# New durations in a list planner: three chained layers on one NeuronCore

## The chip, the cores and the metric

The kernel runs on one core of one Trainium2 chip. The metric is the device time of one execution in microseconds (us); several runs are summed up by their median. One more execution was profiled, and its trace gives the start and end of every instruction. The engines are TensorE (PE, matrix products), VectorE (DVE), ScalarE (ACT), GpSimd (POOL) and SyncE (SP), which here issues all transfers.

## What is computed

Three layers in a row, all in float32. A retention layer (linear attention whose state decays by a factor per head) takes q, k and v of 4 batches, 8 heads, 768 steps and a head size of 64. Its output, as 3072 tokens of 512 features, goes through two layers that widen to 2048 and come back to 512, the first with h·cos(h), the second with an ELU:

```python
for t in range(S):
    state = gamma[None, :, None, None] * state + np.einsum('bhd,bhe->bhde', k[:, :, t], v[:, :, t])
    y[:, :, t] = scale * np.einsum('bhd,bhde->bhe', q[:, :, t], state)
...
h = x @ w_in            # first layer
x = (h * np.cos(h)) @ w_out
h = x @ w_in2           # second layer
x = np.where(h > 0.0, h, np.exp(np.minimum(h, 0.0)) - 1.0) @ w_out2
```

## The kernel before

**Arithmetic.** Every float32 operand of a large product is split into a high and a low part that PE takes at full rate, and three products of parts (`PARTS`) make one. The splits are a copy on ACT (the high part) and a subtraction on DVE (the low part). The projection back in layer one and both products of layer two use a scheme of seven products on halves of the operands in place of eight, and sums and differences of halves before and after (numbers 1 to 7 in the code).

**Stages in time.** Attention works on 24 units of 128 steps of a batch: `scores` (L536, L547), `carried` (L598) and `values` (L629) are small products of 64 by 64; DVE masks the scores (L563) and keeps the state (L572, L575, L578). They are woven into `hidden`, the first hidden layer (L679, 12 matmuls at a time, up to some 340 us). `project` for layer one follows (L925, to 580 us), then `hidden2`, the second hidden layer (L755, 580 to 820 us), then `project` for layer two (L925, to the end). Weights come as 64-bit numbers and are turned into float32 by two ACT and two DVE steps each half (L374, L377), stored, loaded again and split in `prepare` (L431 for the low part).

**Layer two's hidden stage**, to which the prediction comes most, runs 24 steps, each of seven products of six matmuls. Product sums stand in PSUM: three `eg` tiles of two banks each, used as six halves (`bank`), and two `f` tiles of one bank. `seven` issues, in a fixed order, the products of a new step, of the one before it (`mid`) and of the one before that (`old`). A sum that is built up further is copied out by ACT in between (`snap`, `h<-eg`), and DVE later adds the copy to another sum (`c<-eg,h`). The ELU (`elu`) is a chain of ACT steps (L332) and DVE steps (L844, L854, L857).

**The planner.** Nothing is issued by hand. Each step is handed to `Plan.op` with its engine, a duration in us, what it reads and writes, and a lag that shifts its place for buffers. `deadlines` runs PE's steps end to end in program order and gives every other step a due time from those that need it. `run` then plays the program through with these durations: PE keeps program order; DVE, ACT, POOL and SP take, whenever free, the ready step with the earliest due time. Steps marked "ANY" go to DVE or POOL, whichever is free first, with one duration for each. While a DVE and a POOL step run that both use the shared port, both advance at `SHARED` = 0.54 of their rate. A result reaches another engine after `HOP` = 0.2 us. The order in which steps start in this play is the order in which they are written into the program, and so the order on each engine; the tile framework adds the waits by that order.

ACT steps have the line of a helper, L332, and sums and differences on DVE or POOL have L337; the tiles tell them apart: `w<-c` is a weight split, `hl<-ld` an operand's split, `hl<-f` attention's output, `ld<-ld,w` the scaling of a unit's q and k.

Of the kernel before, what the change touches and what calls it, by code (L numbers as in the profile page):

```python
# [299 lines left out]
def retention_then_two_mlps(ctx: ExitStack, tc: tile.TileContext, attn, tab, weights, out):  # L300
# [49 lines left out]
    def to_f32(layer, io, j, lag):  # L350
# [4 lines left out]
        for hh in range(2):  # L355
# [7 lines left out]
                0.65, lambda lo=lo, hi=hi: t.t[:, lo:hi], lambda raw=raw: raw.t[:, :, 1].bitcast(F32),  # L363
# [4 lines left out]
                0.65, lambda: signs.bitcast(F16).rearrange("p (n w) -> p n w", w=2)[:, :, 1],  # L368
# [3 lines left out]
            def steps(lo=lo, hi=hi, raw=raw):  # L372
                u = lambda: t.t[:, lo:hi].bitcast(U32)
                plan.op("DVE", 0.69, lambda: nc.vector.scalar_tensor_tensor(  # L374
                    out=u(), in0=u(), scalar=3, in1=signs, op0=ALU.logical_shift_left, op1=ALU.bitwise_or,
                ), [t[lo, hi], signs_b], [t[lo, hi]], lag)
                plan.op("DVE", 0.69, lambda: nc.vector.scalar_tensor_tensor(  # L377
# [14 lines left out]
    def first_weights(j, lag=0):  # L392
        t = to_f32(0, 0, j, lag)
        n = 4 * j
        while n < 4 * j + 4:
# [7 lines left out]
            act(0.1 + 0.26 * c, high, src, [t[lo, hi]], [span], lag=lag)  # L403
            tt("DVE", 0.08 + 0.29 * c, low, src, lambda high=high: high().bitcast(F32), ALU.subtract,
# [13 lines left out]
    def prepare(layer, io, j, lag=0):  # L418
# [20 lines left out]
        for o, a, b, op in (  # L439
# [4 lines left out]
            tt("ANY", (0.35, 0.7), view(o), view(a), view(b), op, [a, b], [o], lag=lag)  # L444
# [70 lines left out]
    def scores(n):  # L515
# [40 lines left out]
        plan.op("PE", 1.05 if c else 1.2, go, [u], [sc])  # L556
# [11 lines left out]
        plan.op("DVE", 0.68 if c else 0.95, mask, [sc, fall_at], [pt], -80)  # L568
        ds = lambda slot: sc.t[:, :, wid + slot * P:wid + (slot + 1) * P]
        pair = lambda x: x.rearrange("p (e a) d -> p e (a d)", e=2)  # L570
        if c == 0:
            plan.op("DVE", 0.42, lambda: after(nc.vector.tensor_copy(out=pair(state(batch)), in_=ds(0))),  # L572
                    [sc], [state_at(batch)], -40)
            return
        plan.op("DVE", 0.42, lambda: after(nc.vector.tensor_tensor(  # L575
            out=pair(mid(n)), in0=ds(0), in1=pair(aged(n)), op=ALU.add)), [sc, aged_at(n)], [mid_at(n)], -80)
        if c < UPB - 1:
            plan.op("DVE", 0.42, lambda: after(nc.vector.tensor_tensor(  # L578
# [6 lines left out]
    def carried(n):  # L585
# [19 lines left out]
        plan.op("PE", 0.6, go, [u[0, 512], mid_at(n), aged_at(n)], xps)  # L605
# [11 lines left out]
    def values(n):  # L617
# [20 lines left out]
        plan.op("PE", 0.6 if c else 0.8, go, [u[1024, 1536], pt] + ([fence_b[n]] if c else []), xps)  # L638
# [4 lines left out]
        for e in range(2):  # L643
            part = lambda x, e=e: x.t.rearrange("p (a e) t -> p e a t", e=2)[:, e, :, col]
            at = ((b * 2 + e) * P // 2, (b * 2 + e + 1) * P // 2)
            act(0.37, lambda part=part: part(xh), lambda e=e: xps[e].t, [xps[e]], [xh[at]], lag=-80)
            tt("DVE", 0.42, lambda part=part: part(xl), lambda e=e: xps[e].t,
# [10 lines left out]
    def differences(x, y, u, t4, t4_at, wid, lag):  # L658
# [4 lines left out]
        for o, a, b in todo:  # L663
            tt("ANY", (0.62, 1.25), view(o), view(a), view(b), ALU.subtract, [a, b], [o], lag=lag)


    def hidden(blk, j, between=()):
# [30 lines left out]
        act(1.0, n, lambda: h.t, [h], [u], scale=1.0 / TWO_PI)  # L698
# [35 lines left out]
    def load_x2(sb, p, lag=0):  # L734
# [5 lines left out]
        act(1.03, lambda: x.t[:, 0], lambda: t.t, [t], [x[0]], lag=-60)  # L740
        tt("DVE", 1.22, lambda: x.t[:, 1], lambda: t.t, lambda: x.t[:, 0].bitcast(F32), ALU.subtract,
# [40 lines left out]
    def seven(new, mid, old):  # L782
# [393 lines left out]
```

## Time and profile before

| | before |
|---|---|
| median of 3 runs | 1059.04 us (1056.94 to 1061.01) |
| the profiled execution | 1058.54 us |
| its span, first to last instruction | 1056.8 us |
| PE busy | 1028.8 us, 97% |
| DVE busy, instructions | 806.6 us, 76%, 931 |
| ACT busy, instructions | 651.5 us, 62%, 788 |
| POOL busy, instructions | 230.8 us, 22%, 213 |
| chain of work that ended last | PE 26%, DVE 1% of the span; from 766 us on |
| transfers | 323.4 MB, 306 GB/s |

A busy time is the union of an engine's instructions. Matmuls overlap in their pipeline, so one of 128x512 reads as some 390 ns where one starts every 0.23 us. The idle time ahead of an instruction, and what ended it, stand in brackets in a timeline.

### The profile page before, as it was taken

Reading aid. Unit: us, or ns where it says so; the run is one execution under the profiler, and the core shown is the slowest. Engines: PE = TensorE matmul, PEld = TensorE weight load, DVE = VectorE, ACT = ScalarE, POOL = GpSimd, SP = SyncE. Lnnn points to the kernel's source line nnn. Section 1 sums busy time; section 2 is a strip of 40 time slices with the busy share of each in tenths; the row PEclk is TensorE's granted clock in tenths of the full one; section 3 lists DMA queues with packets and bytes.
Section 4 is the critical chain, followed back from the end, with each engine's and each line's share of the span. In section 5 each row is a group of like instructions: output and inputs, shape, how many; then the busy total and the mean of one; then the engine's idle time right before and its main releaser. Section 6 shows DMA issues by size and latency. Waiting matters only on the chain. (4 is left out here: it accounts for less than half of the span.)

```text
span 1056.8 us, 18290 instructions
## 1 busy us (share of the span) xinstructions
PE 1028.8 (97%) x7204; PEld 832.6 (79%) x7208; DVE 806.6 (76%) x931; ACT 651.5 (62%) x788; POOL 230.8 (22%) x213
## 2 busy tenths in 40 slices
PE   6999999999999999999999999999999999999998
PEld 4667788888888888888888777877778888888886
DVE  5898888888889968657468997878889966466453
ACT  2686567766799753443445877877879743544442
POOL 1222340144224610000001542233334201000000
PEclk9899999999999999999999999999999999999999
DMA  9778799999999999999995668789869999999861
GB/s 347 263 259 302 245 361 314 333 355 356 347 331 352 332 345 347 318 326 383 316 359 195 226 245 304 284 311 338 298 239 299 357 333 351 343 320 323 309 209 70
DMA packets 110101, 323.40 MB, mean 306 GB/s; under 512 B 8640, under 2 KB 8640, under 8 KB 107456
## 3 DMA queue, kind: packets, MB, share of 16 engines
q1 hardware_dynamic: 110016, 322.25, 85.4%
q8 instruction: 56, 0.92, 0.4%
q14 instruction: 29, 0.24, 0.1%
HBM read 195.86 MB, written 126.35 MB: 305 GB/s over the span
## 5 line engine op out<-in xcount | busy, mean ns | idle before, releaser
L925 PE MATMUL eg<-hl,w 128*128 128x512 f32 x2016 | 457.9, 389 | 1.0 <-DVE h L877 0.9
L925 PEld LDWEIGHTS eg<-hl,w 128*128 128x128 f32 x2016 | 378.3, 188 | 80.3 <-DVE h L877 1.4
L332 ACT ACTIVATE hl<-ld 128x1024 fp32r<-128x1024 f32 x168 | 177.7, 1060 | 226.3 <-PE eg L925 206.3
L337 DVE TENSOR_TENSOR hl<-ld,hl 128x1024 fp32r<-128x1024 f32 x168 | 211.6, 1269 | 94.4 <-ACT hl L332 94.3
L679 PE MATMUL eg<-hl,w 128*128 128x512 f32 x1152 | 277.0, 397 | 3.0 <-DVE c L704 1.5
L337 POOL TENSOR_TENSOR c<-c 128x512 f32<-128x512 f32 (+1 forms) x141 | 173.3, 1240 | 479.5 <-DVE c L337 170.4
L332 ACT ACTIVATE c<-c 128x1024 f32<-128x1024 f32 (+1 forms) x256 | 232.1, 918 | 57.7 <-DVE c L699 27.9
L679 PEld LDWEIGHTS eg<-hl,w 128*128 128x128 f32 x1152 | 214.2, 189 | 51.5 <-DVE w L337 1.9
L337 DVE TENSOR_TENSOR c<-c 128x512 f32<-128x512 f32 (+2 forms) x127 | 92.8, 741 | 40.5 <-DMA c<-d 30.0
L332 ACT ACTIVATE c<-eg 128x1024 int32<-128x1024 f32 (+2 forms) x95 | 86.3, 909 | 50.7 <-PE eg L679 43.2
L755 PE MATMUL eg<-hl,w 128*128 128x512 f32 x432 | 110.6, 392 | 2.8 <-DVE c L337 1.4
L755 PEld LDWEIGHTS eg<-hl,w 128*128 128x128 f32 x432 | 80.2, 188 | 23.4 <-DVE c L337 3.0
L755 PE MATMUL eg<-ld,w 128*128 128x512 f32 x288 | 74.1, 393 | 4.6 <-ACT h L332 3.9
L699 DVE SCALAR_TENSOR_TENSOR c<-eg,c 128x1024 f32<-128x1024 f32 x48 | 58.6, 1220 | 19.2 <-ACT c L332 17.1
L755 PEld LDWEIGHTS eg<-ld,w 128*128 128x128 f32 x288 | 53.4, 188 | 18.4 <-ACT h L332 6.0
L704 DVE SCALAR_TENSOR_TENSOR c<-c,eg 128x1024 f32<-128x1024 f32 x48 | 58.3, 1215 | 12.1 <-ACT c L332 11.7
L332 ACT ACTIVATE w<-c 128x1024 fp32r<-128x1024 f32 (+3 forms) x59 | 52.7, 920 | 10.0 <-DMA c<-d 3.6
L431 DVE SCALAR_TENSOR_TENSOR w<-c,w 128x768 fp32r<-128x768 f32 (+1 forms) x48 | 56.2, 1183 | 0.9 <-ACT w L332 0.9
L332 ACT ACTIVATE signs<-c 128x512 f16<-128x512 f32 x64 | 50.2, 785 | 6.5 <-DVE c L374 5.8
L377 DVE SCALAR_TENSOR_TENSOR c<-c 128x512 uint32<-128x512 uint32 x64 | 52.6, 831 | 0.7
L374 DVE SCALAR_TENSOR_TENSOR c<-c,signs 128x512 uint32<-128x512 uint32 x64 | 50.2, 785 | 0.8 <-ACT signs L332 0.5
L332 ACT ACTIVATE h<-eg 128x512 f32<-128x512 f32 (+1 forms) x50 | 29.2, 584 | 29.1 <-PE eg L755 10.7
(58 smaller groups left out, 641.8 us busy)
## 6 DMA issues: line engine op xcount, KB each, us to landing
d<-c SPq DMA_DIRECT2D x205, 512.0 KB, 5.1
ld<-d SPq DMA_DIRECT2D x84, 1024.0 KB, 8.1
c<-d SPq DMA_DIRECT2D x93, 512.0 KB, 6.1
c<-in_weights SPq DMA_DIRECT2D x64, 512.0 KB, 6.6
ld<-in_attn SPq DMA_DIRECT2D x20, 1024.0 KB, 7.8
d<-h SPq DMA_DIRECT2D x32, 256.0 KB, 8.3
out<-c SPq DMA_DIRECT2D x11, 512.0 KB, 7.2
d<-c SPq DMA_DIRECT2D x16, 256.0 KB, 3.8
```

The lines of the kernel that those rows point to most:

```text
L332: plan.op("ACT", us, lambda: nc.scalar.activation(out=out_(), in_=in_(), func=func, **kw), r, w, lag)
L337: return e.tensor_tensor(out=out_(), in0=a(), in1=b(), op=op)
L374: plan.op("DVE", 0.69, lambda: nc.vector.scalar_tensor_tensor(out=u(), in0=u(), scalar=3, in1=signs, op0=ALU.logical_shift_left, op1=ALU.b ...
L377: plan.op("DVE", 0.69, lambda: nc.vector.scalar_tensor_tensor(out=u(), in0=raw.t[:, :, 0], scalar=29, in1=u(), op0=ALU.logical_shift_right ...
L431: plan.op("DVE", 0.08 + 0.29 * (hi - lo), lambda: nc.vector.scalar_tensor_tensor(out=w.t[:, lo:hi, 1, :], in0=view(), scalar=turn, in1=hig ...
L679: nc.tensor.matmul(out=h.t[:, half * TB:(half + 1) * TB], lhsT=quarter(j, qd, wpart, kc % 2), rhs=(xh, xl)[xpart].t[:, kc, :], start=(n == ...
L699: plan.op("DVE", 1.22, lambda: nc.vector.scalar_tensor_tensor(out=g.t, in0=h.t, scalar=1.0 / TWO_PI, in1=n(), op0=ALU.mult, op1=ALU.subtra ...
L704: plan.op("DVE", 1.22, lambda: nc.vector.scalar_tensor_tensor(out=g.t, in0=g.t, scalar=1.0, in1=h.t, op0=ALU.subtract, op1=ALU.mult,), [h, ...
L755: nc.tensor.matmul(out=out_(), lhsT=w.t[:, i, wpart, kc * P:(kc + 1) * P], rhs=x.t[:, xpart, kc, :], start=(start and n == 0), stop=(n == ...
L925: nc.tensor.matmul(out=acc.t[:, i * TB:(i + 1) * TB], lhsT=w[:, A_OF[p], wpart, i * P:(i + 1) * P], rhs=hl.t[:, gpart, k, :], start=(p in ...
```

## The change

The numbers in the plan's calls are replaced; no step is added, taken away or rewritten. Below is the core of the diff: the weight steps and splits, the small PE products, the sums and copies of the two hidden stages and the projection. The same is done to the other steps of these kinds.

```diff
-                0.65, lambda: signs.bitcast(F16).rearrange("p (n w) -> p n w", w=2)[:, :, 1],
+                0.64, lambda: signs.bitcast(F16).rearrange("p (n w) -> p n w", w=2)[:, :, 1],
...
-                plan.op("DVE", 0.69, lambda: nc.vector.scalar_tensor_tensor(
+                plan.op("DVE", 0.61, lambda: nc.vector.scalar_tensor_tensor(
...
-            act(0.1 + 0.26 * (hi - lo), high, view, [at], [w[lo, hi]], lag=lag, scale=turn)
-            plan.op("DVE", 0.08 + 0.29 * (hi - lo), lambda: nc.vector.scalar_tensor_tensor(
+            act(0.1 + 0.215 * (hi - lo), high, view, [at], [w[lo, hi]], lag=lag, scale=turn)
+            plan.op("DVE", 0.065 + 0.267 * (hi - lo), lambda: nc.vector.scalar_tensor_tensor(
...
-            tt("ANY", (0.36, 0.75), lambda: aged(n), lambda: state(b), lambda: g_tab().to_broadcast([P, NPAIR, D]),
+            tt("ANY", (0.33, 0.57), lambda: aged(n), lambda: state(b), lambda: g_tab().to_broadcast([P, NPAIR, D]),
...
-        plan.op("PE", 1.05 if c else 1.2, go, [u], [sc])
+        plan.op("PE", 0.65 if c else 0.75, go, [u], [sc])
...
-        plan.op("PE", 0.6, go, [u[0, 512], mid_at(n), aged_at(n)], xps)
+        plan.op("PE", 0.45, go, [u[0, 512], mid_at(n), aged_at(n)], xps)
...
-        plan.op("PE", 0.6 if c else 0.8, go, [u[1024, 1536], pt] + ([fence_b[n]] if c else []), xps)
+        plan.op("PE", 0.4 if c else 0.45, go, [u[1024, 1536], pt] + ([fence_b[n]] if c else []), xps)
...
-        plan.op("DVE", 1.22, lambda: nc.vector.scalar_tensor_tensor(
+        plan.op("DVE", 1.14, lambda: nc.vector.scalar_tensor_tensor(
...
-            act(0.6, lambda: t.t, src, [r], [t], lag=-60)
+            act(0.49, lambda: t.t, src, [r], [t], lag=-60)
...
-            tt("DVE", 0.7, lambda: mid.x.t[:, TB:], E(mid), lambda: mid.s5.t, ALU.add,
+            tt("DVE", 0.6, lambda: mid.x.t[:, TB:], E(mid), lambda: mid.s5.t, ALU.add,
...
-                    act(1.03, lambda hl=hl: hl.t[:, 0], src, [at], [hl[0]])
-                    tt("DVE", 1.22, lambda hl=hl: hl.t[:, 1], src, lambda hl=hl: hl.t[:, 0].bitcast(F32),
+                    act(0.965, lambda hl=hl: hl.t[:, 0], src, [at], [hl[0]])
+                    tt("DVE", 1.14, lambda hl=hl: hl.t[:, 1], src, lambda hl=hl: hl.t[:, 0].bitcast(F32),
...
-        tt("ANY", (1.24, 2.3), lambda: o.t, lambda: a.t, lambda: b.t, ALU.subtract, [a, b], [o], lag=25)
+        tt("ANY", (1.14, 2.4), lambda: o.t, lambda: a.t, lambda: b.t, ALU.subtract, [a, b], [o], lag=25)
```

PE's instructions keep their order word for word. The other orders differ almost everywhere after the first fifteen rows; three places follow, each first as it was and then as it is. Buffer numbers differ between the two programs.

ACT, the copy that the product at 623.81 us of the trace waits for. It is `h_6183<-eg_5945` before and `h_6151<-eg_5946` now. `w<-c` is a weight split, `signs` and `c<-c` 128x512 are weight steps or the start of an ELU.

```order
L332 ACTIVATE h_6128<-f_6062 128x512
L332 ACTIVATE h_6133<-eg_5959 128x512
L332 ACTIVATE c_6135<-c_6116 128x1024
L332 ACTIVATE c_6135<-c_6135 128x1024
L332 ACTIVATE signs_81<-c_6119 128x512
L332 ACTIVATE c_6119<-c_5970 128x512
L332 ACTIVATE w_6037<-c_6130 128x4x256
L332 ACTIVATE h_6183<-eg_5945 128x512
```

```order
L332 ACTIVATE h_6127<-eg_5967 128x512
L332 ACTIVATE h_6129<-f_6070 128x512
L332 ACTIVATE c_6137<-c_6112 128x1024
L332 ACTIVATE c_6137<-c_6137 128x1024
L332 ACTIVATE h_6151<-eg_5946 128x512
L332 ACTIVATE w_6029<-c_6089 128x4x256
```

The copy now stands ahead of the split, and two weight steps that stood before it have moved behind.

PE, five products of layer two's hidden stage, 597 to 604 us in the trace, with the engines whose semaphores they wait for. `eg_5834` before is `eg_5837` now, `eg_5959` is `eg_5967`.

```order
L755 MATMUL f_5989<-ld_5746,w_5804 128x512 [waits DVE_49]
L755 MATMUL f_5989<-ld_5746,w_5804 128x512 x5
L755 MATMUL eg_5834<-hl_5866,w_5785 128x512 x6
L755 MATMUL f_5898<-hl_5876,w_5785 128x512 x6
L755 MATMUL eg_5959<-ld_5841,w_5804 128x512 [waits Activation_49]
```

```order
L755 MATMUL f_5992<-ld_5746,w_5804 128x512 [waits DVE_49]
L755 MATMUL f_5992<-ld_5746,w_5804 128x512 x5
L755 MATMUL eg_5837<-hl_5866,w_5785 128x512 [waits Activation_49]
L755 MATMUL eg_5837<-hl_5866,w_5785 128x512 x5
L755 MATMUL f_5894<-hl_5877,w_5785 128x512 x6
L755 MATMUL eg_5967<-ld_5856,w_5804 128x512 x6
```

The second `eg` product of these waited for no engine and now waits for ACT, which reads the other half of its tile; the last one waited for ACT and now waits for nothing.

DVE, the sum that the product at 793.39 us waits for: `c_7603<-eg_5834,h_7530` before, `c_7622<-eg_5837,h_7540` now. L431 is a weight split, L844, L854 and L857 are ELU steps, `c<-c` 128x256 a sum of weight quarters.

```order
L857 SCALAR_TENSOR_TENSOR c_7474<-c_7533,c_7474 128x512
L854 SCALAR_TENSOR_TENSOR c_7474<-c_7533,eg_5959 128x512
L337 TENSOR_TENSOR c_7590<-c_7509 128x256
L844 SCALAR_TENSOR_TENSOR c_7519<-c_7556,c_7519 128x1024
L337 TENSOR_TENSOR c_7603<-eg_5834,h_7530 128x512
```

```order
L844 SCALAR_TENSOR_TENSOR c_7529<-c_7554,c_7529 128x1024
L337 TENSOR_TENSOR c_7557<-c_7493 128x256
L337 TENSOR_TENSOR c_7557<-c_7493,c_7557 128x256
L431 SCALAR_TENSOR_TENSOR w_7545<-c_7477,w_7545 128x3x256
L431 SCALAR_TENSOR_TENSOR w_7595<-c_7493,w_7595 128x3x256
L854 SCALAR_TENSOR_TENSOR c_7571<-c_7583,eg_5946 128x512
L337 TENSOR_TENSOR c_7622<-eg_5837,h_7540 128x512
```

Two splits, an ELU step and one more quarter sum have come between that chain step (L844) and the sum.

## Rows read from the trace of the kernel before

**Rows 1.** Stretches: length; PE, PEld, DVE, ACT, POOL busy; clock; DMA; GB/s.

```profile
0.00:30.00 30.00, 19.33 (x560) 12.33 (x568) 18.00 (x32) 10.30 (x20) 5.89 (x9) 0.94 0.93 339
30.00:110.00 80.00, 76.40 (x1062) 59.33 (x1052) 71.54 (x97) 57.68 (x80) 18.79 (x24) 0.96 0.73 261
110.00:580.00 470.00, 469.53 (x3582) 384.44 (x3581) 368.54 (x419) 284.17 (x322) 104.39 (x100) 1.00 0.93 331
580.00:820.00 240.00, 231.74 (x999) 185.58 (x998) 208.85 (x258) 193.13 (x262) 88.26 (x73) 1.00 0.78 283
```

**Rows 2.** PE's waits at L755: for whom; us in total, times, longest.

```profile
PE eg L755 <- ACT h L332: 4.8, 6, 1.5
...
PE eg L755 <- DVE c L337: 2.1, 4, 0.7
...
PE f L755 <- DVE hl L337: 0.6, 1, 0.6
...
PE f L755 <- ACT h L332: 0.3, 1, 0.3
PE eg L755 <- ACT c L332: 0.2, 1, 0.2
```

**Rows 3.** Timeline (start, length, engine, line, tiles, idle before): the longest wait.

```profile
621.75 1.06 ACT L332 ACTIVATE w<-c 128x1024 fp32r<-128x1024 f32 x1 [2.24 <-DVE c L337]
...
623.16 0.60 ACT L332 ACTIVATE h<-eg 128x512 f32<-128x512 f32 x1 [0.35 <-DVE c L337]
...
623.81 1.66 PE L755 MATMUL eg<-ld,w 128*128 128x512 f32 x6 [1.46 <-ACT h L332]
```

**Rows 4.** Timeline: three products and the copy of the first one's half.

```profile
602.42 1.52 PE L755 MATMUL eg<-ld,w 128*128 128x512 f32 x6
...
605.14 1.52 PE L755 MATMUL eg<-ld,w 128*128 128x512 f32 x6
...
606.70 0.60 ACT L332 ACTIVATE h<-eg 128x512 f32<-128x512 f32 x1
```

**Rows 5.** Timeline: two weight steps on DVE beside POOL, and alone.

```profile
41.71 2.74 POOL L337 TENSOR_TENSOR ld<-ld,w 128x512 f32<-128x512 f32 x2
42.60 2.40 DVE L377 SCALAR_TENSOR_TENSOR c<-c 128x512 uint32<-128x512 uint32 x2
...
44.92 0.68 DVE L374 SCALAR_TENSOR_TENSOR c<-c,signs 128x512 uint32<-128x512 uint32 x1
...
59.25 1.28 DVE L377 SCALAR_TENSOR_TENSOR c<-c 128x512 uint32<-128x512 uint32 x2
```

**Rows 6.** Timeline: PE's scores of a later unit, and what follows them.

```profile
230.36 0.65 PE L536 MATMUL eg<-ld 64*64 64x64 f32 x32
...
231.41 1.43 PE L679 MATMUL eg<-hl,w 128*128 128x512 f32 x5
```

**Rows 7.** Timeline: three more of nine waits, the first and the last among them.

```profile
59.39 0.69 PE L536 MATMUL eg<-ld 64*64 64x64 f32 x32 [0.91 <-DVE w L578]
...
70.85 0.70 PE L679 MATMUL eg<-hl,w 128*128 128x512 f32 x2 [0.71 <-DVE c L704]
...
742.22 1.65 PE L755 MATMUL f<-hl,w 128*128 128x512 f32 x6 [0.32 <-ACT h L332]
```

**Rows 8.** Timeline: the scores of unit 4, and a carried part with DVE.

```profile
29.42 2.29 DVE L337 TENSOR_TENSOR w<-c,w 128x1024 fp32r<-128x1024 f32 x1
29.55 0.69 PE L536 MATMUL eg<-ld 64*64 64x64 f32 x32 [0.38 <-DVE ld L337]
...
69.45 0.69 PE L598 MATMUL f<-ld,w 64*64 64x64 f32 x32
69.50 1.20 DVE L704 SCALAR_TENSOR_TENSOR c<-c,eg 128x1024 f32<-128x1024 f32 x1
...
70.63 1.16 DVE L337 TENSOR_TENSOR w<-c,w 128x768 fp32r<-128x768 f32 x1
```

**Rows 9.** Timeline: a sum on DVE and its product; the first projection.

```profile
792.66 0.68 DVE L337 TENSOR_TENSOR c<-eg,h 128x512 f32<-128x512 f32 x1
...
793.39 1.66 PE L755 MATMUL eg<-ld,w 128*128 128x512 f32 x6
...
822.51 1.75 PE L925 MATMUL eg<-hl,w 128*128 128x512 f32 x7
```

More of the change, by code (lines that the diff above doesn't have):

```diff
@@ L373, in steps @@
                 u = lambda: t.t[:, lo:hi].bitcast(U32)
[L374 removed]
+                plan.op("DVE", 0.61, lambda: nc.vector.scalar_tensor_tensor(
                     out=u(), in0=u(), scalar=3, in1=signs, op0=ALU.logical_shift_left, op1=ALU.bitwise_or,
                 ), [t[lo, hi], signs_b], [t[lo, hi]], lag)
[L377 removed]
+                plan.op("DVE", 0.61, lambda: nc.vector.scalar_tensor_tensor(
                     out=u(), in0=raw.t[:, :, 0], scalar=29, in1=u(),
@@ L402, in first_weights @@
             low = lambda k=k, i=i, c=c: win1[k].t[:, i:i + c, 1, :]
-            act(0.1 + 0.26 * c, high, src, [t[lo, hi]], [span], lag=lag)
-            tt("DVE", 0.08 + 0.29 * c, low, src, lambda high=high: high().bitcast(F32), ALU.subtract,
+            act(0.1 + 0.215 * c, high, src, [t[lo, hi]], [span], lag=lag)
+            tt("DVE", 0.065 + 0.267 * c, low, src, lambda high=high: high().bitcast(F32), ALU.subtract,
                [t[lo, hi], span], [span], lag=lag)
@@ L566, in mask @@
                 in1=fall()[:, :, 0:wid // HC, :], op=ALU.mult))
-        plan.op("DVE", 0.68 if c else 0.95, mask, [sc, fall_at], [pt], -80)
+        plan.op("DVE", 0.6 if c else 0.95, mask, [sc, fall_at], [pt], -80)
         ds = lambda slot: sc.t[:, :, wid + slot * P:wid + (slot + 1) * P]
@@ L571, in scores @@
         if c == 0:
-            plan.op("DVE", 0.42, lambda: after(nc.vector.tensor_copy(out=pair(state(batch)), in_=ds(0))),
+            plan.op("DVE", 0.33, lambda: after(nc.vector.tensor_copy(out=pair(state(batch)), in_=ds(0))),
                     [sc], [state_at(batch)], -40)
             return
-        plan.op("DVE", 0.42, lambda: after(nc.vector.tensor_tensor(
+        plan.op("DVE", 0.33, lambda: after(nc.vector.tensor_tensor(
             out=pair(mid(n)), in0=ds(0), in1=pair(aged(n)), op=ALU.add)), [sc, aged_at(n)], [mid_at(n)], -80)
         if c < UPB - 1:
-            plan.op("DVE", 0.42, lambda: after(nc.vector.tensor_tensor(
+            plan.op("DVE", 0.33, lambda: after(nc.vector.tensor_tensor(
                 out=pair(state(batch)), in0=ds(1), in1=pair(mid(n)), op=ALU.add)),
@@ L645, in values @@
             at = ((b * 2 + e) * P // 2, (b * 2 + e + 1) * P // 2)
-            act(0.37, lambda part=part: part(xh), lambda e=e: xps[e].t, [xps[e]], [xh[at]], lag=-80)
-            tt("DVE", 0.42, lambda part=part: part(xl), lambda e=e: xps[e].t,
+            act(0.263, lambda part=part: part(xh), lambda e=e: xps[e].t, [xps[e]], [xh[at]], lag=-80)
+            tt("DVE", 0.33, lambda part=part: part(xl), lambda e=e: xps[e].t,
                lambda part=part: part(xh).bitcast(F32), ALU.subtract, [xps[e], xh[at]], [xl[at]], lag=-80)
@@ L739, in load_x2 @@
         dma(4, lambda: t.t.rearrange("p k t -> p (k t)"), lambda: x2d[sb].t[:, i], [x2d[sb][i]], [t], lag)
-        act(1.03, lambda: x.t[:, 0], lambda: t.t, [t], [x[0]], lag=-60)
-        tt("DVE", 1.22, lambda: x.t[:, 1], lambda: t.t, lambda: x.t[:, 0].bitcast(F32), ALU.subtract,
+        act(0.965, lambda: x.t[:, 0], lambda: t.t, [t], [x[0]], lag=-60)
+        tt("DVE", 1.14, lambda: x.t[:, 1], lambda: t.t, lambda: x.t[:, 0].bitcast(F32), ALU.subtract,
            [t, x[0]], [x[1]], lag=-60)
@@ L823, in seven @@
             product(mid, 7, E(mid), False, e_at(mid))
-            tt("DVE", 0.7, lambda: mid.x.t[:, TB:], E(mid), lambda: mid.s5.t, ALU.add,
+            tt("DVE", 0.6, lambda: mid.x.t[:, TB:], E(mid), lambda: mid.s5.t, ALU.add,
                [e_at(mid), mid.s5], [mid.x[TB, 2 * TB]])
             product(mid, 3, Fv(mid), False, mid.f)
-            tt("DVE", 0.7, lambda: mid.x.t[:, 0:TB], Fv(mid), lambda: mid.s6.t, ALU.add,
+            tt("DVE", 0.6, lambda: mid.x.t[:, 0:TB], Fv(mid), lambda: mid.s6.t, ALU.add,
                [mid.f, mid.s6], [mid.x[0, TB]])
@@ L834, in seven @@
             product(mid, 2, G(mid), True, g_at(mid))
-            tt("DVE", 0.7, lambda: mid.y.t[:, TB:], G(mid), lambda: mid.s1.t, ALU.add,
+            tt("DVE", 0.6, lambda: mid.y.t[:, TB:], G(mid), lambda: mid.s1.t, ALU.add,
                [g_at(mid), mid.s1], [mid.y[TB, 2 * TB]])
@@ L841, in elu @@
         if which == "x":
-            act(1.03, lambda: u.t, lambda: x.t, [x], [u], func=AF.Relu, scale=-1.0)
-            act(1.03, lambda: u.t, lambda: u.t, [u], [u], func=AF.Exp, scale=-1.0)
-            plan.op("DVE", 1.25, lambda: nc.vector.scalar_tensor_tensor(
+            act(0.965, lambda: u.t, lambda: x.t, [x], [u], func=AF.Relu, scale=-1.0)
+            act(0.965, lambda: u.t, lambda: u.t, [u], [u], func=AF.Exp, scale=-1.0)
+            plan.op("DVE", 1.14, lambda: nc.vector.scalar_tensor_tensor(
                 out=x.t, in0=u.t, scalar=1.0, in1=x.t, op0=ALU.subtract, op1=ALU.max,
@@ L876, in last_half @@
             if piece:
-                plan.op("DVE", 0.42, lambda src=src, lo=lo, hi=hi: nc.vector.tensor_copy(
+                plan.op("DVE", 0.33, lambda src=src, lo=lo, hi=hi: nc.vector.tensor_copy(
                     out=c.t[:, lo:hi], in_=src()), [at], [c[lo, hi]])
@@ L896, in total @@
             t = Buf("c", [P, 2 * TB])
-            tt("DVE", 1.22, lambda: t.t, lambda: buf.t, lambda: s.t, ALU.add, [buf, s], [t])
+            tt("DVE", 1.14, lambda: t.t, lambda: buf.t, lambda: s.t, ALU.add, [buf, s], [t])
             return t
```

28 lines of the change are left out of this document (14 added, 14 removed).

## The prediction

> **What bounds the kernel now.** I read the busy times stage by stage first. TensorE (PE) is busy to 0.5 us in the 470 us from 110 to 580, and in the other stages it is idle for 10.7 us before 30, 3.6 us from 30 to 110 and 8.3 us from 580 to 820 [rows 1]. DVE, at 208.9 of 240 us, and ACT, at 193.1, are near their own limit only in that last stage [rows 1]. So the bound is PE's own work, and a new order on the other engines can change nothing but PE's idle time: 12.3 us between 30 and 820, and part of the 10.7 us before it, whose larger share waits for the first loads and a stall that the trace gives no releaser. What can be lost has no such limit.
>
> The list of PE's waits comes next. In the second hidden stage (L755, 168 products of six matmuls) it names 13 waits, ten of them for ACT's copies `h<-eg` or DVE's sums [rows 2]. Then the timeline at the longest: the copy that the product at 623.81 needs begins at 623.16, right behind a weight split of 1.06 us on ACT, and PE stands for 1.46 us [rows 3].
>
> One thing must be seen before the order can be read. The sums of that stage lie in halves of three `eg` tiles of two banks, and waits are kept by the tile, not by the half. A product at 602.42 ends at 603.94; the copy that reads its half could start then, but starts at 606.70, 0.04 us behind the end of the product at 605.14, which writes the other half [rows 4]. Which of the two waits is settled by which one the planner starts first. So the planner's clock, which the change corrects, moves waits as well as instructions.
>
> **The change, part by part.** PE's instructions keep their order, and no instruction is added or removed. All that moves is the order on DVE, ACT, POOL and the queue of transfers, 18 more operations on DVE and 18 fewer on POOL (69 go one way, 51 the other), and who waits for whom.
>
> The corrected numbers of DVE and ACT agree with the trace: two weight steps in a row end after 1.28 us where the first takes 0.68, so they start 0.60 apart, and the table now says 0.61 where it said 0.69 [rows 5]. Those of the small PE products do not: the scores of a later unit take 1.05 us from start to start, and the table goes from 1.05 to 0.65 [rows 6]. As PE's order is fixed and later due times shift alike, I cost that at nothing. If the shift does count, it lets attention's steps go ahead of others, and that is in the terms below.
>
> *Waits that lose their cause.* At nine places the instruction that PE waited for now stands further ahead on its engine, or the wait itself is gone from the order. They run from 59.39 (0.91 us, the state's sum on DVE, now ahead of three others) through 70.85 and the short wait behind it (0.71 and 0.28), 586.19 (0.73), 591.62 (0.61), 612.53 (0.43), 623.81 (1.46) and 737.53 (0.62) to 742.22 (0.32) [rows 3, 7]. Together 6.1 us. At 623.81 the split moves behind the copy (first place of the order shown above), and the sum on DVE that frees the copy's buffer moves up too. What is late next there is the product's other operand, on hand for some twenty us. So I take all of it, and zero as the other end.
>
> *Waits that may come.* At nine other places more stands ahead of what PE waits for, by durations of the trace less the time PE had to spare:
> - 29.55, scores of unit 4: the split of 2.29 us that ran behind DVE's scaling goes ahead of it [rows 8]; alone it takes about 1.3. About 0.8 us of PE idle just behind goes, so 0.5.
> - 69.45, carried part: a step of 1.20 us (L704) and a split of 1.16 go ahead of the sums that free its PSUM tile [rows 8]; 0.9 to spare, so 1.4.
> - Three lesser ones (the hidden block at 123, the one at 271, the product at 583.8): 2.3 together.
> - 684 to 698: two ACT steps, of 1.05 and some 0.6 to 0.8 us, ahead of a copy: 1.6. At 717, three of them: 2.2.
> - 793.39, with 0.05 us to spare [rows 9]: two splits, an ELU step and a subtraction that was on POOL now stand ahead of the sum it waits for (third place of the order): 2.4.
> - 822.51, the first projection [rows 9]: a split and former POOL work ahead of its operand: 1.6.
>
> Together 12.0 us if nothing in front of these instructions finds idle time, nothing if all does. As nearest measure I take the waits of the trace itself: 34 product waits for ACT or DVE leave at most two other products between the sum that is read and the product that waits, and 13 cost idle time [rows 2], 0.38. So 4.6 us. The new order has 44 such waits, though hardly fewer waits in all (119 for 121), so the measure is rather low than high.
>
> *The move from POOL to DVE.* While POOL works on two scalings of 2.74 us together, two weight steps take 2.40 us on DVE, against 1.28 us alone [rows 5]. An operation taken off POOL thus gives DVE back about what it adds, 0.6 us, and I put nothing for it beyond the places named. The Trainium skill says otherwise (SBUF — State Buffer, Who interferes with whom): the shared port pair is an exclusive lock, and the loser blocks fully, for the whole instruction. The rows show slowed instructions, 1.1 us lost beside 2.7 us of POOL, not a full stop. By the rule the last two places of the list would cost nothing, and the time would be 1.5 us less.
>
> *The transfers.* Loads and stores trade places on the one queue, mostly by one, and in 110 to 580 PE shows no gap for it [rows 1]. Nothing for it; if a load of the last projection, which lands just in time, falls behind a store, it is one store, about 1.5 us.
>
> **The sum.** The profiled execution took 1058.54 us; less 6.1, plus 4.6, is 1057.0. The median of the runs lies 0.5 above that execution, so 1057.5. No change to speak of: a measurement here tells about 0.5%, 5.3 us, from none.
>
> **The rivals.**
> - *The new waits cost in full.* Place: products from 684 on and the first projection, where DVE and ACT run full and cannot catch up. For it: DVE at 208.9 of 240 us, and ten more tight waits. Against it: 13 of 34 were all that cost before, and one backlog pays for several places. With half of the gain lost too (the next reader late in turn), 1058.5 - 3.0 + 12.0 + 0.5 = 1068. It is slower by over 0.5% once the added exceed the removed by 5.3 us. Chance 0.13.
> - *The planner's clock now fits, and the new tight waits are met.* Then 1058.5 - 6.1 + 0.5 = 1053.0, 0.57% faster. For it: the new numbers are those of the rows, so a step planned to end in time does. Against it: the planner still knows nothing of the two halves sharing a tile. Chance 0.12.
> - *The order moves and PE does not notice.* Losses and gains under 1 us: 1059. For it: 470 us without a gap under the same kind of order. Against it: 8.3 us of idle hang on single places of ACT's and DVE's order. It is within 0.5%, with chance 0.25; my forecast has 0.50.
>
> **How the numbers follow.** Faster 0.12, same 0.75 (forecast and third rival, 1053.8 to 1064.2), slower 0.13. The range takes in both ends of the added waits, 0 and 12.0, against the 6.1: 1053.0 to 1065.0.
>
> **What would show it.** Right: the 1.46 us before 623.81 is gone, PE's idle from 580 to 820 is 5 to 9 us, made of other places than before, several on products that waited for nothing; 110 to 580 stays under 1.5 us; POOL is busy some 15 us less, DVE within 10 us of before. Wrong: idle over 13 us in that stage, or under 3; or the granted clock of a stretch that was at 2.4 GHz falls to 1.2 because PE stood longer at 29 or 69.

## The result: 1.35% slower

The changed kernel takes 1074.15 us in the median (1071.09 to 1078.45), the kernel before 1060.03 in the same runs: a ratio of 1.0135, 95% interval 1.0087 to 1.0184. The forecast was 1057.5 in a range of 1053 to 1065, so it failed in size and in sign. The span of the profiled execution went from 1056.8 to 1072.6 us.

Part 1 of the page of the changed kernel (busy time, share, instructions): DVE has gained 5.7 us of work and POOL has lost 21.0, as the order showed. PE's busy time has gone up by 7.0 us with the same matmuls.

```profile
span 1072.6 us, 18304 instructions
PE 1035.8 (97%) x7208; PEld 837.6 (78%) x7208; DVE 812.3 (76%) x949; ACT 653.0 (61%) x788; POOL 209.8 (20%) x195
```

The stretches of [rows 1], now in the changed kernel:

```profile
0.00:30.00 30.00, 18.25 (x468) 11.06 (x471) 16.29 (x27) 8.08 (x14) 5.03 (x8) 0.89 0.93 340
30.00:110.00 80.00, 75.92 (x1122) 59.79 (x1119) 72.95 (x104) 59.37 (x83) 17.95 (x21) 0.98 0.75 266
110.00:580.00 470.00, 465.53 (x3591) 380.62 (x3583) 361.06 (x422) 279.83 (x319) 84.37 (x87) 0.99 0.91 325
580.00:820.00 240.00, 228.83 (x969) 182.70 (x968) 211.28 (x261) 186.72 (x252) 79.53 (x64) 0.98 0.76 278
```

From 110 to 580 us PE is now idle for 4.5 us, where it was 0.5, and the clock column has left 1.00 in two stretches. Set against each other by the same instruction, PE is 0.4 us later than before at the scores of 59.39 [rows 7], 8.45 later at the carried part that started at 276.94 us before (by chance a product shown below has the same figure in the changed kernel), still 8.45 at the first product of the second hidden stage (580.16), and 16.1 at the first projection of layer two [rows 9]. So the time goes in two stages: 8.45 us in attention, 7.7 in the second hidden stage. In the first, 5.6 us are more idle time, in the second 3.2; the other 7.4 us are the same work taking longer, most of it at the lower clock. Three places hold most of it.

**First place, attention.** PE's rows, and DVE's ahead of them, in the timeline of the changed kernel (start, length, engine, line, tiles, in brackets the idle time before and what ended it):

```profile
259.94 0.57 SPq L327 DMA_DIRECT2D ld<-in_attn  x1
...
270.41 1.22 DVE L699 SCALAR_TENSOR_TENSOR c<-eg,c 128x1024 f32<-128x1024 f32 x1
...
271.55 1.53 DVE L337 TENSOR_TENSOR ld<-ld,w 128x512 f32<-128x512 f32 x2
...
273.13 0.46 PE L536 MATMUL eg<-ld 64*64 64x64 f32 x16 [0.96 <-DVE ld L337]
...
275.57 1.22 DVE L704 SCALAR_TENSOR_TENSOR c<-c,eg 128x1024 f32<-128x1024 f32 x1
...
276.94 8.52 PE L679 MATMUL eg<-hl,w 128*128 128x512 f32 x24 [2.88 <-DVE c L704]
```

The unit's load goes out at 259.94 and lands at 269.87; before it went out at 254.35 and landed at 262.67. Its two scalings run on DVE at 271.55, the cosine step that frees PE's tile is later still, and the 24 matmuls behind the wait take 8.52 us, where 24 take 5.74 at full clock. The stretches around them show why (length, busy times, then the clock): it falls to 0.50, the lower of its two levels (1.2 GHz), behind PE's idle time, and is back at 1.00 in the row from 283.

```profile
271.00:277.00 6.00, 2.16 (x84) 1.56 (x82) 5.39 (x8) 4.76 (x7) 2.21 (x2) 0.92 0.93 337
277.00:281.00 4.00, 4.00 (x10) 3.13 (x11) 3.37 (x6) 1.87 (x4) 0.00 (x0) 0.50 0.99 338
...
283.00:286.00 3.00, 3.00 (x43) 2.23 (x41) 0.00 (x0) 0.50 (x1) 0.00 (x0) 1.00 0.86 345
...
595.20:600.40 5.20, 5.14 (x12) 4.08 (x13) 5.20 (x4) 2.38 (x4) 2.86 (x1) 0.51 0.95 334
...
613.70:617.70 4.00, 3.91 (x10) 3.10 (x11) 3.40 (x5) 3.72 (x5) 0.52 (x1) 0.57 0.02 4
```

The last two of these rows belong to the other two places.

**Second place, the third product of the second hidden stage** (the expectations below call it the sixth, and the thirteenth the fourteenth), in the same timeline:

```profile
588.11 5.52 POOL L337 TENSOR_TENSOR c<-c 128x256 f32<-128x256 f32 x1 [6.78 <-DVE c L337]
...
591.84 1.21 DVE L337 TENSOR_TENSOR ld<-c,ld 128x1024 fp32r<-128x1024 f32 x1
593.66 2.67 SPq L327 DMA_DIRECT2D c<-d  x4
593.66 1.06 ACT L332 ACTIVATE w<-c 128x1024 fp32r<-128x1024 f32 x1 [2.01 <-POOL c L337]
594.62 0.58 ACT L332 ACTIVATE h<-eg 128x512 f32<-128x512 f32 x1
...
595.26 5.36 PE L755 MATMUL eg<-ld,w 128*128 128x512 f32 x12 [3.76 <-ACT h L332]
```

A sum of weight quarters takes 5.52 us on POOL (0.74 in the median of the 53 of its size). It ends 0.58 us behind the DVE step at 591.84, the last of a row of DVE steps without a break: six of them started one behind the other after 588.11. ACT's weight split waits for it, and the copy that PE needs stands behind the split.

**Third place, the thirteenth product:**

```profile
609.16 1.28 ACT L332 ACT_TABLE_LOAD   x1
610.46 1.06 ACT L332 ACTIVATE c<-c 128x1024 f32<-128x1024 f32 x1
611.42 0.82 ACT L332 ACTIVATE w<-c 128x768 fp32r<-128x768 f32 x1
...
613.15 0.58 ACT L332 ACTIVATE c<-eg 128x512 f32<-128x512 f32 x1
...
613.79 2.79 PE L755 MATMUL eg<-hl,w 128*128 128x512 f32 x6 [2.19 <-ACT c L332]
```

This is the product of the second order shown ahead, that "waited for no engine and now waits for ACT". I had shown that wait and not priced it. The list of waits at L755, for [rows 2]:

```profile
PE eg L755 <- ACT h L332: 6.8, 6, 3.8
PE eg L755 <- ACT c L332: 2.2, 1, 2.2
PE eg L755 <- DVE c L337: 2.1, 4, 0.6
```

Eleven waits of 11.1 us, where it was thirteen of 8.0.

### The profile page after: what moved, and what is told of

It is laid out like the page before. It is cut to its first block, busy times and chain, and to the rows that moved or that the text cites. A ratio compares the mean times of both kernels' runs of the same rounds, so it can differ in the third digit from the quotient of the medians.

```text
span 1072.6 us, 18304 instructions
## 1 busy us (share of the span) xinstructions
PE 1035.8 (97%) x7208; PEld 837.6 (78%) x7208; DVE 812.3 (76%) x949; ACT 653.0 (61%) x788; POOL 209.8 (20%) x195
## 4 chain that ended last, share of the span: by engine, by line
PE 80%; ACT 7%; DVE 6%; DMA 4%; issue 3%; POOL 1%; SPq 0%; DVEq 0%; ACTq 0%; POOLq 0%
PE eg L925 41%; PE eg L679 23%; PE eg L755 9%; ACT c L332 4%; PE f L755 3%; DVE c L337 2%; DMA ld<-in_attn 1%; ACT h L332 1%; PE f L629 1%; PE f L598 1%; DMA c<-in_weights 1%; PE eg L547 1%; PE eg L536 1%; DMA d<-c 1%; DMA c<-d 1%
## 5 line engine op out<-in xcount | busy, mean ns | idle before, releaser
L337 POOL TENSOR_TENSOR c<-c 128x512 f32<-128x512 f32 (+2 forms) x130 | 157.1, 1216 | 583.6 <-DMA c<-d 256.3
L755 PE MATMUL eg<-hl,w 128*128 128x512 f32 x432 | 112.4, 396 | 4.9 <-ACT c L332 2.2
L755 PEld LDWEIGHTS eg<-hl,w 128*128 128x128 f32 x432 | 80.5, 189 | 26.8 <-ACT c L332 4.1
L755 PE MATMUL eg<-ld,w 128*128 128x512 f32 x288 | 76.5, 403 | 6.5 <-ACT h L332 5.7
L755 PEld LDWEIGHTS eg<-ld,w 128*128 128x128 f32 x288 | 54.9, 193 | 21.5 <-ACT h L332 8.5
L699 DVE SCALAR_TENSOR_TENSOR c<-eg,c 128x1024 f32<-128x1024 f32 x48 | 58.5, 1220 | 13.3 <-ACT c L332 11.9
L431 DVE SCALAR_TENSOR_TENSOR w<-c,w 128x768 fp32r<-128x768 f32 (+1 forms) x48 | 54.7, 1156 | 2.1 <-ACT w L332 2.0
L377 DVE SCALAR_TENSOR_TENSOR c<-c 128x512 uint32<-128x512 uint32 x64 | 50.1, 789 | 1.2
```

The costliest lines, as they stand in the source:

```text
L337: return e.tensor_tensor(out=out_(), in0=a(), in1=b(), op=op)
L377: plan.op("DVE", 0.61, lambda: nc.vector.scalar_tensor_tensor(out=u(), in0=raw.t[:, :, 0], scalar=29, in1=u(), op0=ALU.logical_shift_right ...
L431: plan.op("DVE", 0.065 + 0.267 * (hi - lo), lambda: nc.vector.scalar_tensor_tensor(out=w.t[:, lo:hi, 1, :], in0=view(), scalar=turn, in1=h ...
L699: plan.op("DVE", 1.14, lambda: nc.vector.scalar_tensor_tensor(out=g.t, in0=h.t, scalar=1.0 / TWO_PI, in1=n(), op0=ALU.mult, op1=ALU.subtra ...
L755: nc.tensor.matmul(out=out_(), lhsT=w.t[:, i, wpart, kc * P:(kc + 1) * P], rhs=x.t[:, xpart, kc, :], start=(start and n == 0), stop=(n == ...
```

## The experiments

In this table "attention" is how much later than before PE starts the carried part of 276.94, and "second hidden" how much it loses from there to the first projection of layer two, less what is lost between 276.94 and 580.16 (in brackets where it isn't zero). The opening with its first loads differs from run to run: the three kernels with the order of the changed kernel up to that point show +8.5, +11.3 and +6.7 there, so that column is good to some 2.5 us either way; the other repeats within 1.

| kernel | median, us | ratio, 95% interval | attention | second hidden |
|---|---|---|---|---|
| changed | 1074.15 | 1.0135 [1.0087, 1.0184] | +8.5 | +7.7 |
| pe_only | 1064.87 | 1.0046 [1.0028, 1.0063] | +6.1 | -0.8 |
| not_pe | 1065.69 | 1.0053 [1.0033, 1.0074] | -1.2 | +7.8 |
| any_only | 1064.64 | 1.0041 [1.0019, 1.0063] | +4.0 | +1.0 |
| dve_act | 1067.18 | 1.0067 [1.0041, 1.0092] | -0.6 | +9.3 |
| c_only | 1075.30 | 1.0131 [1.0092, 1.0169] | +11.3 | +6.1 |
| b_only | 1069.38 | 1.0083 [1.0051, 1.0114] | +6.7 | +4.5 |
| not_pe_b | 1060.88 | 1.0009 [0.9991, 1.0027] | -2.4 | +4.3 |
| a_chain | 1071.34 | 1.0097 [1.0064, 1.0129] | +4.1 (+1.6) | +8.0 |
| b_moves | 1058.88 | 0.9994 [0.9982, 1.0007] | -0.6 | -0.4 |
| n_mm | 1067.10 | 1.0063 [1.0041, 1.0085] | +1.5 | +7.5 |
| n_x99 | 1068.73 | 1.0083 [1.0064, 1.0101] | +5.1 (+0.9) | +4.5 |
| n_hop19 | 1067.83 | 1.0066 [1.0042, 1.0090] | +4.8 | +6.2 |
| a_mm | 1074.67 | 1.0136 [1.0115, 1.0156] | +4.6 (+2.0) | +7.4 |
| a_hop19 | 1078.41 | 1.0170 [1.0145, 1.0195] | +6.7 (+3.4) | +11.2 |
| a_x99 | 1068.75 | 1.0081 [1.0054, 1.0108] | +6.9 | +5.4 |

### The change in two halves

The two stages can be told apart cleanly: PE's small products exist in attention alone, and from the second hidden stage on the order of pe_only is that of before, and that of not_pe the changed kernel's, step for step.

pe_only, made from the kernel before:

```diff
-        plan.op("PE", 1.05 if c else 1.2, go, [u], [sc])
+        plan.op("PE", 0.65 if c else 0.75, go, [u], [sc])
-        plan.op("PE", 0.6, go, [u[0, 512], mid_at(n), aged_at(n)], xps)
+        plan.op("PE", 0.45, go, [u[0, 512], mid_at(n), aged_at(n)], xps)
-        plan.op("PE", 0.6 if c else 0.8, go, [u[1024, 1536], pt] + ([fence_b[n]] if c else []), xps)
+        plan.op("PE", 0.4 if c else 0.45, go, [u[1024, 1536], pt] + ([fence_b[n]] if c else []), xps)
```

> The kernel before with only the three durations of PE's small products changed. From the second hidden stage on, its order is that of the kernel before, step for step; only the attention stage is ordered anew. Theory P (the short PE durations make the planner think attention runs faster than it does, so loads and scalings come too late for PE): some 1068 us (1065 to 1070), PE's idle time between 250 and 300 us about 4 to 5 us with a stretch at half clock behind it, as in the changed kernel; 580 to 820 as before, 8 us of idle. Theory D (PE's order is fixed and its due times shift alike, so these three numbers cost nothing; the loss is the new order of DVE and ACT): 1060 us, as before.

not_pe is the changed kernel with these three lines put back.

> The changed kernel with the three durations of PE's small products put back. From the second hidden stage on, its order is that of the changed kernel, step for step. Theory P: the loss of the attention stage (8.5 us by 300 us of the trace) goes, that of the second hidden stage (5 to 7 us) stays: some 1066 us (1064 to 1068), with PE's waits of about 3.8 and 2.2 us at its sixth and fourteenth product of that stage still there. Theory D: 1073 to 1075, nothing gained.

Both came out as theory P has it, pe_only a little below its range and with 3.6 us of idle time at the place for some 4 to 5: 4.9 and 5.7 us over before, each clear of it. PE's timeline of pe_only has the stall again:

```profile
272.20 0.46 PE L536 MATMUL eg<-ld 64*64 64x64 f32 x16 [0.89 <-DVE ld L337]
...
275.79 4.54 PE L679 MATMUL eg<-hl,w 128*128 128x512 f32 x12 [2.66 <-DVE c L704]
```

and that of not_pe has no wait there:

```profile
269.26 0.41 PE L536 MATMUL eg<-ld 64*64 64x64 f32 x16
269.49 0.65 PE L547 MATMUL eg<-ld 64*64 64x64 f32 x32
270.07 5.74 PE L679 MATMUL eg<-hl,w 128*128 128x512 f32 x24
```

So the three numbers that I had costed at nothing make the stall at 277 us. How they do it is an argument from the planner's own play. Played with the short numbers, PE idles for 2.1 us ahead of these scores and 2.1 behind them, which it doesn't with the old ones: with 0.68 us too little for the three products of a unit together, PE runs ahead of the loads and of the other engines' steps, and their order is made for that race. The play of before stays 2.5 to 8 us ahead of the trace from 60 us to the end; that of the changed kernel is 8 us ahead at 60, 28 at 308 and 46 at the end. No run took the transfers by themselves.

### One step at each place

These kernels plan as the kernel that they are made from and then change the planned list by hand before it is written out.

b_only, one sum taken from POOL to DVE (1636 is its number in the plan):

```diff
+        acts = [(n, "DVE" if n == 1636 else eng, None if n == 1636 else behind) for n, eng, behind in acts]
```

> The changed kernel with one operation moved from POOL to DVE: the sum of weight quarters that took 5.52 us on POOL at 588.11 us while DVE worked without a break. Theory S (DVE's stream shuts POOL out of the shared port, ACT's split waits for POOL's sum, and the copy that PE needs stands behind that split): the split and the copy start some 2 us earlier, PE's wait of 3.76 us falls to about 2, bound then by the subtraction on DVE that ends near 593; 2 us less, 1072, or 4 less if the clock stays at full speed. Rival (the copy is late for ACT's and DVE's own backlog): under 0.5 us.

```profile
589.71 1.04 ACT L332 ACTIVATE w<-c 128x1024 fp32r<-128x1024 f32 x1
590.65 0.59 ACT L332 ACTIVATE h<-eg 128x512 f32<-128x512 f32 x1
...
591.29 3.09 PE L755 MATMUL eg<-ld,w 128*128 128x512 f32 x12 [1.53 <-ACT h L332]
...
594.04 7.44 POOL L337 TENSOR_TENSOR c<-c 128x1024 f32<-128x1024 f32 x1 [14.56 <-DVE c L337]
```

ACT's split no longer waits, PE's wait falls from 3.76 to 1.53 us, its twelve matmuls take 3.09 in place of 5.36, and the kernel is 4.8 us faster in the median: theory S, a little over its upper end. The intervals of the two kernels overlap; the trace shows the gain at its place (4.5 us lost in the second hidden stage for 7.7), and the next pair of runs repeats it. The next POOL step, a subtraction of twice the usual width, is held up in its turn for 7.44 us (2.42 where it runs free, in the same trace), with nobody waiting for it.

not_pe_b has the same edit on not_pe.

> The changed kernel with the three PE durations put back and with the one sum of weight quarters moved from POOL to DVE. Theory S (both losses are apart in time and add): the 4.5 us that this move gained from the sixth to the twelfth product of the second hidden stage come off the 1065.7 of the kernel with PE's durations put back: 1061, within 2 us of the kernel before. Rival (with another start the queue of POOL and DVE falls differently and POOL is not shut out there): 1065.

It gave 1060.88, level with before (0.9991 to 1.0027) and clear of not_pe. The two repairs add: 8.5 and 4.8 us by themselves, 13.3 together. The two losses of 4.9 and 5.7 us fall short of the 14.1 of the whole change, by no more than the intervals allow. Level in time isn't free of loss: the profiled execution still loses 4.3 us in the second hidden stage and is 2.4 ahead in attention, where not_pe, with the same order, was 1.2 ahead.

c_only, one product written ahead of the ACT step that reads the other half of its tile:

```diff
+        at = {a[0]: i for i, a in enumerate(acts)}
+        acts.insert(at[1754], acts.pop(at[1768]))
```

> The changed kernel with one line of the program moved: the product at 613.79 us is written ahead of the ACT copy that reads the other half of its tile. No engine's own order changes; one wait on ACT moves from this product to the one two places later, whose true need it is. Theory T (the wait between halves of a tile is false and its 2.2 us of idle, with the stretch at half clock behind it, are lost to it alone): the idle time there goes, the clock stays at full speed, 3 to 4 us less: 1070 to 1071. Rival (ACT is late anyway and the next product waits as long): within 1 us of 1074, the same idle one or two products later.

The rival was right. The wait is gone at its place and stands four products later:

```profile
614.19 1.52 PE L755 MATMUL eg<-hl,w 128*128 128x512 f32 x6
...
621.80 1.66 PE L755 MATMUL eg<-ld,w 128*128 128x512 f32 x6 [2.01 <-ACT h L332]
```

PE's stretch around it is 1.7 us shorter than in the changed kernel, since here the clock stays up, but the time is that of the changed kernel within what the runs can tell. ACT was late by itself: in the changed kernel it runs without a break from 610.46 behind a table load of 1.28 us that the plan doesn't hold. No run took that load away, and the kernel before has the same one at 597.40 with no wait at this product, so why ACT is late here stays open. The false wait between halves was real, and taking it away gained nothing.

a_chain, seven steps of the first place moved ahead (the load, its scalings, four cosine steps):

```diff
+        for n, m in ((870, 835), (875, 806), (876, 806), (935, 807), (936, 962), (937, 962), (938, 945)):
+            i = next(i for i, a in enumerate(acts) if a[0] == n)
+            j = next(i for i, a in enumerate(acts) if a[0] == m)
+            acts.insert(j, acts.pop(i))
```

> The changed kernel with seven steps of one place moved ahead on their own engines: the load of the unit whose scores start at 273.13 us by six places in the queue of transfers, its two scalings on DVE ahead of two weight steps, and the four cosine steps that free the tile which the product at 276.94 waits for (two on DVE, two on ACT). Theory P (that stall is the planner's order at this place, made for a PE that runs attention faster than it does): the idle times of 0.96 and 2.88 us shrink to under 1 together and the clock stays at full speed; 5 us less, 1069. Rival (DVE and ACT have fallen behind as a whole, and what is moved back is late next): the idle time turns up at the products or scores of the next 20 us, within 1.5 us of 1074.

Between the two: the scores no longer wait, and of what is lost from 257.98 on 3.1 us come back by 370 us, but the block behind still waits 2.22 us, and the next unit's scores, which didn't wait, now do for 0.63.

```profile
272.29 0.41 PE L536 MATMUL eg<-ld 64*64 64x64 f32 x16
...
275.38 5.69 PE L679 MATMUL eg<-hl,w 128*128 128x512 f32 x24 [2.22 <-DVE c L704]
...
289.01 0.46 PE L536 MATMUL eg<-ld 64*64 64x64 f32 x16 [0.63 <-DVE ld L337]
```

### Numbers or a new order?

any_only changes the four pairs for DVE or POOL alone, dve_act the numbers of the fixed DVE and ACT steps alone.

> The kernel before with only the four pairs of durations of the steps that may run on DVE or POOL changed. Theory U (the old, longer numbers of DVE and ACT stood in for time the planner does not know of, such as the shared port and the loading of ACT's table; the loss of the second hidden stage comes from cutting them): within 2 us of before, 1058 to 1062. Rival L (each new order costs or gains some us by chance): anything from 1055 to 1066, as likely slower as the next.

> The kernel before with only the durations of the steps fixed to DVE or ACT changed (PE's and the pairs for DVE or POOL stay). Theory U: the loss of the second hidden stage is here, 5 to 7 us from 580 to 830 us, 1064 to 1067, and the planner's own play of that stage ends some 6 us or more ahead of the trace. Rival L: the loss need not be here; anything from 1055 to 1066, with stalls at other products than the sixth and the fourteenth.

dve_act came out a little above theory U (1067.2, with 9.3 us lost in the second hidden stage), and any_only did not fit it: it lost 4 us in attention, at places of its own. Every part of the change was slower than before, which pointed to theory L. Three draws that say nothing new of the hardware test it:

```diff
-MM = 0.2268
+MM = 0.2267
```

> A draw that says nothing of the hardware: the kernel before with the planner's time of one matmul 0.2267 in place of 0.2268 us. From row 212 of 2975 on nearly every order but PE's changes all the same. Theory N (the order follows what the numbers say, and numbers that say the same cost the same): within 2 us of before, 1058 to 1062. Theory L (the order of before is one of the better of many that near numbers give, and any new order costs some us by the places where it stalls, whatever the numbers): 1062 to 1068, with stalls at other products than before.

```diff
+        us = us if eng in ("PE", "SP") else tuple(0.99 * x for x in us) if eng == "ANY" else 0.99 * us
         self.ops.append((eng, us, fn, deps, bufs, news, n + lag))
```

> A second draw: the kernel before with every duration of DVE, ACT and POOL taken at 0.99 of what it was, PE's and the transfers' as they were. Theory N: 1058 to 1062. Theory L: 1062 to 1068, stalls at other places again.

```diff
-HOP = 0.2
+HOP = 0.19
```

> A third draw: the kernel before with 0.19 us in place of 0.2 us from one engine to another in the planner's play. Theory N: 1058 to 1062. Theory L: 1062 to 1068, stalls at other places again. If the three draws lie on both sides of before, neither holds, and the spread of the draws is the measure for what a new order costs or gains by chance.

1067.1, 1068.7 and 1067.8 us: theory L, all three, the second 0.7 us over its range. One ten-thousandth of a microsecond in one number costs 0.63% (0.41% to 0.85%). The waits of n_mm at L755, beside the list above:

```profile
PE eg L755 <- ACT h L332: 4.8, 7, 1.4
PE eg L755 <- DVE c L337: 3.2, 6, 0.8
PE eg L755 <- ACT c L332: 1.5, 1, 1.5
PE f L755 <- DVE ld L337: 1.2, 1, 1.2
```

Then the same three shifts on the changed kernel:

> The changed kernel with the planner's time of one matmul 0.2267 in place of 0.2268 us: a first new order from the new numbers. Theory V (the new numbers cost what any new order costs, some 8 us, and the changed kernel's order is a bad draw): 1066 to 1070. Theory M (the new numbers are worse than a new order alone): 1071 to 1077. In both, if PE's short durations make the stall of the attention stage, PE stands there for 2 us or more between 255 and 290 us, as in the planner's own play (1.7, 1.4 and 1.2 us); if it belongs to one order, it is gone.

> The changed kernel with 0.19 us in place of 0.2 us from one engine to another in the planner's play: a second new order from the new numbers. Here the planner puts the sum of weight quarters that POOL held up on DVE of itself. Theory V: 1066 to 1070. Theory M: 1071 to 1077. Stall of the attention stage as above (2.2 and 1.1 us in the planner's play).

> The changed kernel with every duration of DVE, ACT and POOL at 0.99 of its new number: a third new order from the new numbers; here too that sum is on DVE. Theory V: 1066 to 1070. Theory M: 1071 to 1077. Stall of the attention stage as above (1.2, 1.7 and 1.7 us in the planner's play).

Neither theory holds by itself: two of three are at or above the changed kernel, one is with the draws of the old numbers. The four orders from the new numbers have a mean of 1074.0 us, the three new ones from the old numbers 1067.9. PE's short numbers settle a place: from 257.98 to 276.94 every kernel with them loses 2.1 to 6.9 us, and each of the eight others with the old ones 0.5 or less. They don't settle the 6 us. From 59.39 to 257.98 it is the other way round, the three draws lose 2.9 to 6.5 us and the four kernels 0.4 to 2.5, so that from 59.39 to 276.94 the means are 5.2 and 6.3. In the second hidden stage the four lose 5.4 to 11.2 and the three 4.5 to 7.5, which these few draws don't separate; the rest of the 6 us lies in the opening, between the two stages and at the end.

### Can before be bettered by hand?

b_moves moves nine steps of the kernel before at eight of its waits:

```diff
+        for n, m, behind in ((1719, 1637, 0), (1680, 1780, 1), (1807, 1790, 0), (1820, 1689, 0), (1907, 1896, 0),
+                             (2102, 2080, 0), (2237, 2268, 0), (2330, 2305, 0), (2355, 2345, 0)):
+            a = next(a for a in acts if a[0] == n)
+            acts.remove(a)
+            acts.insert(next(i for i, a in enumerate(acts) if a[0] == m) + behind, a)
```

> The kernel before with its own numbers and nine steps of the second hidden stage moved by hand on ACT or DVE, at eight of its waits (583.81, 612.53, 623.81, 644.18, 697.94, 742.22, 756.66 and 768.40 us in its trace): what PE waits for goes ahead of one to five steps that are due later. Theory R (each stall is one step in the wrong place, and taking it away costs nothing elsewhere): the waits of 0.5, 0.4, 1.5, 0.7, 0.9, 0.3, 0.5 and 0.6 us go, 5.3 together: 1054 to 1055.5 against 1059.4. Rival W (as in the two kernels before where a single wait was taken away, what was moved back is late next): half of it or less, 1057 to 1060, with new waits within some 20 us of the old ones.

1058.88 against 1059.16, a ratio of 0.9994 (0.9982 to 1.0007): rival W. At seven of the eight places the wait is gone, at 623.81 it is 0.30 for 1.46. Others took their place, in PE's timeline:

```profile
585.72 1.66 PE L755 MATMUL eg<-ld,w 128*128 128x512 f32 x6 [1.67 <-ACT h L332]
...
628.12 1.73 PE L755 MATMUL eg<-hl,w 128*128 128x512 f32 x6 [1.95 <-DVE c L854]
```

The first was 0.73 in the kernel before and the second nothing; a third of 0.74 at 743.74 is new as well. The stretch behind the second shows the clock at 0.65:

```profile
628.10:633.00 4.90, 4.88 (x14) 3.88 (x15) 4.80 (x5) 2.79 (x5) 2.06 (x2) 0.65 0.79 319
```

No version here is measurably faster than the kernel before.

## Why the prediction was wrong

- **Waits that lose their cause: right.** All nine are gone from the trace of the changed kernel, 6.1 us.
- **Waits that may come: the failed term.** I took 12.0 us for nine places and 0.38 of that, 4.6. What came is 16.3 us of idle time. Those nine places cost 8.5 (0.24 at 29.55, 0.87 at 69.45, 3.84 at 271, 2.99 at 583.8, 0.51 from 684 to 698, and nothing at 123, 717, 793.39 and 822.51), and places that I hadn't listed another 7.8 (2.19 at the third place, 1.30 at 801.69, 0.97 near 65, and nine of 0.1 to 0.6). So both the factor and the list were at fault. The factor of 13 in 34 was counted in an order of which the draws show that it is a good one; at the nine places 0.70 came. The signs I had named speak for themselves: 580 to 820 us has 11.2 us of idle time and not 5 to 9, 110 to 580 has 4.5 and not under 1.5.
- **The clock stood only in the last line.** It was named for 29 and 69 us and no price was put. It fell at all three large waits, and the matmuls shown behind them took 2.8, 2.3 and 1.1 us longer than as many at full clock above (5.74 in not_pe, 3.09 in b_only, 1.66 in c_only): 6.2 of the 16.1 us.
- **PE's small products "cost at nothing": failed.** The three numbers alone made the kernel 4.9 us slower (pe_only), with the stall at 277 us. "Later due times shift alike" leaves out that the durations of the loads and of the other engines stay as they are while PE's play runs faster. How much of the 4.9 us is due to these numbers and how much to any new order stays open: the three draws lose 2.9 to 6.5 us in attention at other places.
- **"Nothing" for the transfers: not borne out** at the same place, where a load goes out 5.6 us later and the scores of its unit wait 0.96. The 2.88 us behind them hang on cosine steps of ACT and DVE; a_chain moved all of these together, so the load's own share isn't shown. That 110 to 580 had no gap before [rows 1] said nothing of a new order.
- **POOL and DVE: the wrong direction.** From [rows 5], where POOL slows DVE, I priced the moved work at nothing. The loss came from a step that stayed on POOL and that DVE shut out, 4.8 us. The Trainium skill (SBUF — State Buffer, Who interferes with whom) has whoever issues second block fully. The row at 588.11 agrees in that POOL stood, 5.52 us for a step of 0.74, and did so over six DVE steps and not one. By that rule the last two places of my list would cost nothing; they cost nothing, and no run shows whether for that reason. I had set that rule aside for a row of slowed instructions, though the trace of the kernel before has such a step as well, with nobody waiting for it:

```profile
590.25 4.18 POOL L337 TENSOR_TENSOR c<-c 128x256 f32<-128x256 f32 x1 [12.33 <-DMA c<-d]
```

- **The false waits of half tiles: right as a mechanism, and of no weight.** c_only took one away and nothing was gained.
- **The first rival** (the new waits cost in full, 1068, chance 0.13) was the right kind, and still 6 us short, by the clock and by the places not listed. What no case held is that a new order as such costs 8 us here. The cases went from a gain of 6 to a loss of 9 around the old order, as if it were an average one.

What stays open is why the order of before is as good as it is. Eleven other whole orders (the changed kernel's, four from parts of the change, six from empty shifts) were all slower, by 5 to 19 us, and the runs don't tell what sets it apart. One sign of it: of the nine of these with an order of their own in the second hidden stage, eight stand at its thirteenth product for 1.3 to 2.4 us, where the kernel before doesn't wait.

## What to carry to other kernels

Where a planner's numbers set an order, measure first what a change in the fourth digit does: what such empty changes do (here a loss of some 8 us each from the old numbers, and from the new ones anything from a gain of 5 to a loss of 4) is what any edit to the table may do, and only what goes beyond it is the edit's own. A plan needs the time from one step to the next on its engine: the scores had 0.65 us in the table and 1.05 in the trace [rows 6]. The lag of the trace behind the planner's play shows where such a number is. A wait that is taken away at an engine that runs behind comes back some products later, so look for what made that engine late.

## What the runs showed of the hardware

- A POOL step of 0.74 us took 5.52 (5.46 in not_pe, 4.18 in the kernel before), and one of 2.42 took 7.44, while DVE worked on SBUF without a break. Delays of several us are rare: of the 53 sums of the first size in the changed kernel eight took over 1.1 us, and one of these over 2.
- PE's granted clock fell to half behind waits of 2.88, 3.76 and 2.19 us in the changed kernel and of 1.95 in b_moves. It stayed at 1.00 behind 2.22 us in a_chain and 2.01 in c_only, so the length of the wait alone doesn't settle it.
- With the same order on every engine, most of PE's waits repeat to a few hundredths of a microsecond: 0.77, 0.73, 0.61, 0.43 and 1.46 us in the second hidden stage of before, 0.77, 0.73, 0.61, 0.43 and 1.47 in pe_only. Not all do: one of 0.47 was 0.08 in pe_only, and one of 0.41 in the changed kernel was 1.14 in not_pe. What differs most from run to run is the opening.
